# A recurrence in chunks and an ELU MLP on one core: the fourth pair of k heads rides in the unused rows of the other three tiles, so six transposes turn k and not eight

## The chip, the cores and the metric

The kernel runs on one core of a Trainium2 chip. The metric is device microseconds of one execution, from three runs of the kernel before; smaller is better. A profile was taken of one further execution.

## What is computed

The reference, cut to what matters. For each batch and head a 48 x 48 state is carried over 768 tokens; its output goes through a two-layer MLP with an ELU between.

```
B, H, S, D = 4, 8, 768, 48
f = 1 / (1 + exp(-f_logit))
for t in range(S):
    state = f[:, :, t, :, None] * state + einsum('bhd,bhe->bhde', k[:, :, t], v[:, :, t])
    y[:, :, t] = einsum('bhd,bhde->bhe', q[:, :, t], state)
x = y.transpose(0, 2, 1, 3).reshape(B * S, H * D)        # 3072 x 384
h = x @ w_in                                             # 384 -> 2048
out = where(h > 0, h, exp(min(h, 0)) - 1) @ w_out        # 2048 -> 384
```

q, k and f_logit lie in memory with tokens innermost, v with heads next to each other.

## The kernel before

The function `fast` does all the work here; `general` is a fallback that a flag selects, and it is not entered. The tokens are cut into 12 **units** of 256 (three to a batch). A unit passes through two parts: its attention, and sixteen **steps** of MLP. The MLP is the backbone of the program: 12 times 16 steps run in one written-out order (the loop at L1164), where an even step T computes a product with `w_in` (`up`, in `up7` at L883 seven-product form, matmuls at L893) and an odd step a product with `w_out` (`down`, matmuls at L995) for the block two behind. A table `plan` says which pieces of attention are put at which step. TensorE gets its instructions in exactly this order, and so do VectorE, ScalarE, GpSimd and the DMA queue of SP: `manual_schedule` leaves nothing to a scheduler, only the semaphore waits are derived.

**The tiles of q, k and f.** Eight heads of 48 rows make four pairs, and `qkf` holds a tile of 128 partitions x 4 pairs x 256 tokens for each of q, k and f, in two buffers used by alternate units. A pair fills 96 of 128 rows: rows 16 to 111 (`MAIN`); rows 0 to 15 and 112 to 127 (`GAP`) of a pair are unused and zero in q and k. For f the fourth pair is not loaded into a tile of its own at all: its 96 rows are put into the gap rows of the first three pairs (L441), so that the sigmoids, running products and reciprocals take three pairs of 256 columns and not four, and a DMA (`move`, L639) brings the fourth pair's decay to its own place afterwards.

**The pieces of attention of unit u**, with t = 16 (u - 1) as the step where the unit before it starts its MLP:

- `load` (L432) at t - 16: SP issues f, two f gap loads, k, q and v.
- `gates` at t - 8: two activations on ScalarE over f.
- `decays` (L641) at t - 7, t - 5, t - 3: VectorE makes the running product (`grow`, L627) and its reciprocal (`fall`, L632) of pair p, and GpSimd multiplies k and q by them (`scale`, L622, one instruction for each pair of q or k). `settle` at t - 1 does q of the third pair and k and q of the fourth.
- `transposed` (L663) at t + 2: TensorE turns the scaled k, 128 x 128 at a time: four pairs x two windows of 128 tokens, eight transposes (L670), into two PSUM tiles of two pairs each; ScalarE copies each tile to SBUF with one instruction of 128 x 512 (`kn`, L674).
- `both` at t + 5: `advance` (L729) multiplies turned k by v for the state updates, `scores` (L706) multiplies k by q; VectorE masks the scores (L714) and adds up the states (L687).
- `outputs` (L744) at t + 9 and `carried` (L764) at t + 11 make y. Between them ScalarE reads one column of each output bank (`between`, L751), and `carried` waits for that read. ScalarE then copies y to `xt` (L771, L773).

Units 0 and 1 go through a special start, while weights are still being unpacked. Unit 2 has steps of its own: decays at 16, 18, 20 and 22, the transposes at 23, `advance` at 25, `scores` at 26, `outputs` at 27, `carried` at 28; at the same steps VectorE builds combinations of `w_out` (`combine`, L861) for the seven-product form.

At step 4 `warm` (L1050) issues `SMALL` = 16 matmuls of one column each, whose result nobody reads.

An `elu` of a block (L947 on VectorE, then four sums on GpSimd, L957) is issued one block later than its `up`; ScalarE copies one quarter of each `up` product out of PSUM (`u`, L900), VectorE adds it to others (`hh`, L902, L915), and ScalarE takes two activations of the sum (`gg`, L925, L926).

Of the kernel before, what the change touches and what calls it, by code (L numbers as in the profile page):

```python
# [8 lines left out]
FP32 = mybir.dt.float32  # L9
# [347 lines left out]
def fast(ctx: ExitStack, tc: tile.TileContext, q, k, v, f_logit, w_in, w_out, out, flag, outer):  # L357
# [18 lines left out]
    nc = tc.nc  # L376
# [6 lines left out]
    NW = U // W  # L383
# [3 lines left out]
    HP = H // 2  # L387
    NFT = DFF // 128
    NKT = DM // 128
    PAD = 64 - D  # L390
# [5 lines left out]
    WA = 1  # L396
    F1 = (1, 3)
    W0 = 3
    SMALL = 16
    RR = 2  # L400
    HOLD = 2
    A1 = (2, 8, 10, 11)
# [10 lines left out]
    FULL = (slice(0, 64), slice(64, 128))  # L413
    MAIN = slice(PAD, 64 + D)
    GAP = (0, 64 + D)
    assert (D, DM, HP) == (48, 384, NKT + 1) and S % U == 0

    cst = ctx.enter_context(tc.tile_pool(name="cst", bufs=1))
    sb = ctx.enter_context(tc.tile_pool(name="sb", bufs=2))
    ps = ctx.enter_context(tc.tile_pool(name="ps", bufs=1, space=bass.MemoryType.PSUM))  # L420

    NB = 2

    qkf = [
        {n: cst.tile([128, HP, 2, U] if n == "f" else [128, HP, U], FP32, name=f"{n}{i}") for n in "fqk"}
        for i in range(NB)
    ]
    src = {"q": q, "k": k, "f": f_logit}
    vs = [cst.tile([128, NW, PAD + DM + PAD], FP32, name=f"v{i}") for i in range(NB)]
    ats, kns, xts, sts, pys = {}, {}, {}, {}, {}  # L430

    def load(u, names="fkqv"):  # L432
        b, s0 = u // UPB, (u % UPB) * U
        for n in names.replace("v", ""):
            to = qkf[u % NB][n][MAIN]
            frm = src[n][b, :, :, s0 : s0 + U].rearrange("(p r) d s -> (r d) p s", r=2)
            if n == "f":
                to, frm = to[:, 0:NKT, 0], frm[:, 0:NKT]
            nc.sync.dma_start(out=to, in_=frm)
            for r in range(2 if n == "f" else 0):  # L440
                nc.sync.dma_start(  # L441
                    out=qkf[u % NB][n][GAP[r] : GAP[r] + PAD, 0:NKT, 0],
                    in_=src[n][b, 2 * NKT + r, :, s0 : s0 + U].rearrange("(i j) s -> i j s", i=PAD),
                )
        if "v" in names:
            nc.sync.dma_start(
                out=vs[u % NB][:, :, PAD : PAD + DM], in_=v[b, s0 : s0 + U].rearrange("(c t) n -> t c n", t=W)
            )
# [16 lines left out]
    blank(0, nc.vector, nc.gpsimd)  # L465
    blank(1, nc.vector, zeros=nc.gpsimd)
    load(0, "fkq")
    load(1, "f")
    load(0, "v")

    fine = cst.tile([128, NKT, 1], FP32, name="fine")
    nc.vector.memset(fine[:], 1.0)
    first_y = [ps.tile([128, NW, NKT, C], FP32, tag="h", name=f"psY0_{b}", bufs=2) for b in range(2)]
    for y in first_y:
# [7 lines left out]
        out=causal[:], in_=causal[:], compare_op=ALU.is_ge, fill=0.0, base=0,  # L482
# [178 lines left out]
    pts = {}  # L661

    def transposed(u, h, bank, pairs=(0, 1)):  # L663

        if 0 in pairs:
            pts[u, h] = ps.tile([128, 2, NW, 128], FP32, tag=bank, name=f"psT{u}_{h}")
            kns[u, h] = sb.tile([128, 2, NW, 128], FP32, tag="kn", name=f"kn{u}_{h}")
        for p in pairs:
            for w in range(NW):
                nc.tensor.transpose(  # L670
                    pts[u, h][:, p, w], in_=qkf[u % NB]["k"][:, 2 * h + p, w * W : (w + 1) * W], identity=ident[:]
                )
        p = slice(pairs[0], pairs[-1] + 1)
        nc.scalar.copy(kns[u, h][:, p], pts[u, h][:, p])  # L674

    pus = {}

# [41 lines left out]
    def advance(u, pairs=range(HP)):  # L719

        if u not in pus:
            pus[u] = [ps.tile([128, NW, HP, D], FP32, tag=n, name=f"psU{u}_{n}") for n in ("a0", "a1")]
        pu = pus[u]
        for p in pairs:
            for w in range(NW):
                for r in range(2):
                    h = 2 * p + r
                    for b in range(2):
                        nc.tensor.matmul(  # L729
                            pu[b][FULL[r], w, p], lhsT=kns[u, p // 2][FULL[b], p % 2, w, FULL[r]],  # L730
                            rhs=vs[u % NB][FULL[b], w, PAD + h * D : PAD + (h + 1) * D],
                            start=(w == 0 and p == 0), stop=(w == NW - 1 and p == HP - 1), skip_group_check=True,
                        )
# [91 lines left out]
    def at_step(step, *todo):  # L825
        plan.setdefault(step, []).extend(todo)

    def both(u):

        advance(u)  # L830
        mask(u, scores(u, ("m3", "m0")))
        for c in range(NC):
            step(u, c)

    def attention(u, first, then):

        kept = []
        for p, i in enumerate(first):
            at_step(i, (lambda: settle(u)) if p == NKT else lambda p=p: decays(u, p))
        if u > 1:  # L840
            at_step(then[0], lambda: transposed(u, 0, "a0"), lambda: transposed(u, 1, "a1"))
        if len(then) == 4:
            at_step(then[1], lambda: both(u))
        else:
            at_step(then[1], lambda: advance(u))
            at_step(then[2], *(lambda c=c: step(u, c) for c in range(NC)))
            at_step(then[3], lambda: kept.append(scores(u)), lambda: mask(u, kept[0]))
        at_step(then[-2], lambda: outputs(u))
        at_step(then[-1], lambda: carried(u))
# [196 lines left out]
    def warm(n, bank="m0", small=0):  # L1046

        pw = ps.tile([128, 4, 128], FP32, tag=bank, name="psW")
        for _ in range(small):
            nc.tensor.matmul(pw[0:1, 0, 0:1], lhsT=ident[:, 0:1], rhs=ident[:, 0:1], start=True, stop=True)  # L1050
        for _ in range(n):
            nc.tensor.matmul(  # L1052
                pw[:], lhsT=ident[:], rhs=ident[:].unsqueeze(1).broadcast_to([128, 4, 128]), start=True, stop=True
            )
# [8 lines left out]
    for p in range(NKT):  # L1063
        grow(0, p)
        scale(0, ("k", p, nc.gpsimd))
        if p < 2:
            transposed(0, 0, "m0", (p,))
    move(0, 0, nc.scalar)
    transposed(0, 1, "m1", (0,))
    fall(0, 0)  # L1070
    scale(0, ("q", 0, nc.gpsimd))
    warm(WA, "m3")
    gates(1, bias=0)
    advance(0, (0, 1))
    pc = scores(0, ("m2", "m3"), (0,))
    nc.gpsimd.tensor_copy(
# [18 lines left out]
    a = qkf[1]["f"][:, 0:NKT, 0]  # L1095
# [33 lines left out]
    for n in range(1, NFT):  # L1129
        t = min(max(needs[n][0] - 2, 0), n)  # L1130
# [7 lines left out]
    at_step(A1[0], lambda: transposed(1, 0, "a0"), lambda: transposed(1, 1, "a1"))  # L1138
    at_step(4, lambda: warm(0, "m3", SMALL))
    attention(1, (), A1)  # L1140
# [10 lines left out]
    for u in range(3, NU):  # L1151
        t = (u - 1) * NFT
# [5 lines left out]
    for n in range(NR):  # L1158
        t = 3 * NFT + (NU - 4) * NFT * n // NR + RR
# [29 lines left out]
def kernel(tc, q, k, v, f_logit, w_in, w_out, out):  # L1189

    nc = tc.nc
    with tc.tile_pool(name="flags", bufs=1) as pool:
        flag = pool.tile([1, 1], I32, name="flag")
        store = fast(tc, q, k, v, f_logit, w_in, w_out, out, flag, pool)
        seen = nc.values_load(flag[0:1, 0:1])
        with tc.If(seen < 128) as branch:
            general(tc, q, k, v, f_logit, w_in, w_out, out)  # L1200
        with branch.Else():
            store(nc.sync, nc.scalar)
# [32 lines left out]
```

## Time and profile before

| What | Value |
|---|---|
| Three runs | 565.10, 565.82, 567.58 us; median 565.82 us |
| The profiled execution's own time | 565.24 us |
| Its span, first to last instruction | 563.5 us (1.74 us lie around it) |
| PE busy (matmul) | 544.1 us, 97% of the span |
| PE weight loads | 508.7 us, 90% |
| DVE, ACT, POOL busy | 407.1, 228.7, 293.5 us (72%, 41%, 52%) |
| Granted TensorE clock | 0.998 |

PE is TensorE, PEld its weight loads, DVE VectorE, ACT ScalarE, POOL GpSimd and SP the engine that issues most DMAs. A line of the groups names the line of the kernel, engine, operation, output and inputs, shape, count, busy microseconds, mean nanoseconds of one instruction, and the idle time of the engine ahead of them with what ended it. Matmuls are pipelined: each is shown longer than the distance to the next one's start, so the cost of a matmul in a dense stream is read from start to start in the timeline. In a timeline line the two numbers ahead are the start and the length, in microseconds, of a run of like instructions, and the count is at its end; a bracket tells of idle time ahead of it and what ended that.

### The profile page before, as it was taken

What the parts mean: (1) busy time and instruction counts of PE and PEld (TensorE: products, weight loads), DVE (VectorE), ACT (ScalarE), POOL (GpSimd) and SP (SyncE); (2) the same over time, 40 slices, a digit from 0 to 9 for tenths busy, and PEclk for the clock granted to TensorE, in tenths of its full rate; (3) what the DMA queues carried; (4) which work ended last, traced back from release to release, by engine and by line L of the source; (5) the groups of instructions that cost most, each with busy time, mean ns of one, the idle gap of its engine ahead of it and who ended that gap; (6) DMA issues with size and microseconds to landing.
All of it is one profiled execution on the core that took longest, in us unless ns stands there. A gap on an engine that the chain in (4) does not pass through costs nothing.

```text
span 563.5 us, 15590 instructions
## 1 busy us (share of the span) xinstructions
PE 544.1 (97%) x6368; PEld 508.7 (90%) x6368; DVE 407.1 (72%) x802; ACT 228.7 (41%) x424; POOL 293.5 (52%) x567
## 2 busy tenths in 40 slices
PE   7789898999999999999999999999999999999995
PEld 3466677999999999999999999999999999999995
DVE  8789989786676785785785785786686777735553
ACT  3279752434343433434334343343333343333331
POOL 6610779475374374465366367257257348325332
PEclk9999999999999999999999999999999999999999
DMA  8999951024024216216207307307306302201001
GB/s 209 257 250 231 288 150 43 3 52 111 2 51 140 59 33 170 73 20 179 79 10 182 87 10 183 85 9 183 86 9 181 88 9 71 86 4 33 30 2 35
DMA packets 38194, 53.31 MB, mean 95 GB/s; under 512 B 3712, under 2 KB 27936, under 8 KB 38112
## 3 DMA queue, kind: packets, MB, share of 16 engines
q1 hardware_dynamic: 37312, 51.62, 35.6%
q8 instruction: 52, 0.85, 0.6%
q10 hardware_dynamic: 800, 0.59, 0.5%
q14 instruction: 30, 0.25, 0.2%
HBM read 44.04 MB, written 4.72 MB: 87 GB/s over the span
## 4 chain that ended last, share of the span: by engine, by line
PE 84%; DVE 8%; ACT 3%; issue 3%; POOL 1%; DMA 1%; ACTq 0%; DVEq 0%; POOLq 0%
PE psH L893 37%; PE psM L995 36%; PE psU_a L729 2%; PE psS L706 2%; PE psY L744 2%; PE psY L764 2%; PE psT L670 2%; DVE f L632 2%; ACT area L574 1%; PE psW L1052 1%; DVE bits L564 1%; DMA f<-f 1%; DVE area L568 1%; PE psY L809 1%; DVE wi L582 1%
## 5 line engine op out<-in xcount | busy, mean ns | idle before, releaser
L893 PE MATMUL psH<-xt,wi 128*128 128x128 f32 (+1 forms) x1056 | 195.0, 294 | 0.0
L957 POOL TENSOR_TENSOR sums<-gg 128x128 f32<-128x128 f32 x176 | 78.3, 466 | 209.8 <-DVE gg L947 183.8
L925 ACT ACTIVATE gg<-hh 128x512 f32<-128x512 f32 x88 | 55.5, 630 | 252.3 <-DVE hh L915 117.5
L893 PEld LDWEIGHTS psH<-xt,wi 128*128 128x128 f32 x1056 | 149.5, 192 | 1.7 <-DVE hh L902 0.2
L893 PE MATMUL psH<-xt,area 128*128 128x128 f32 x704 | 121.8, 275 | 1.0 <-DVE hh L915 0.7
L893 PEld LDWEIGHTS psH<-xt,area 128*128 128x128 f32 x704 | 106.5, 191 | 6.1 <-PE psH L893 1.1
L902 DVE TENSOR_TENSOR hh<-psH,u 128x256 f32<-128x256 f32 x88 | 37.0, 420 | 101.3 <-ACT u L900 101.3
L995 PE MATMUL psM<-area,sums 128*128 128x192 f32 x528 | 102.2, 326 | 0.0
L995 PEld LDWEIGHTS psM<-area,sums 128*128 128x128 f32 x528 | 88.0, 190 | 0.2 <-issue 0.2
L995 PE MATMUL psM<-wo,gg 128*128 128x192 f32 x352 | 73.9, 332 | 0.0
L947 DVE SCALAR_TENSOR_TENSOR gg<-gg,hh 128x512 f32<-128x512 f32 x88 | 64.1, 728 | 1.5 <-ACT gg L926 1.5
L632 DVE RECIPROCAL f<-f 128x256 f32<-128x256 f32 x36 | 62.8, 1748 | 1.1
L926 ACT ACTIVATE gg<-gg 128x512 f32<-128x512 f32 x96 | 60.6, 631 | 3.0
L995 PEld LDWEIGHTS psM<-wo,gg 128*128 128x128 f32 x352 | 56.2, 190 | 1.4
L915 DVE TENSOR_TENSOR hh<-psH,u43h 128x256 f32<-128x256 f32 (+1 forms) x176 | 54.7, 353 | 3.0
L622 POOL TENSOR_TENSOR q<-q,f 128x256 f32<-128x256 f32 x48 | 38.9, 812 | 21.7 <-DVE f L632 8.7
L957 POOL TENSOR_TENSOR sums<-gg,sums 128x128 f32<-128x128 f32 x88 | 46.3, 527 | 6.9
L622 POOL TENSOR_TENSOR k<-k,f 128x256 f32<-128x256 f32 x48 | 40.5, 847 | 7.7 <-DMA f<-f 5.5
L957 POOL TENSOR_TENSOR sums<-sums,gg 128x128 f32<-128x128 f32 x88 | 43.9, 498 | 0.0
L915 DVE TENSOR_TENSOR u43h<-psH,hh 128x256 f32<-128x256 f32 x88 | 37.0, 420 | 8.9 <-PE psH L893 7.9
L995 PE MATMUL psM<-wo,sums 128*128 128x192 f32 x176 | 43.1, 326 | 0.0
L995 PE MATMUL psM<-area,gg 128*128 128x192 f32 x176 | 43.0, 326 | 0.0
(99 smaller groups left out, 646.9 us busy)
## 6 DMA issues: line engine op xcount, KB each, us to landing
area<-in_moe_w_out_dram SPq DMA_DIRECT2D x8, 768.0 KB, 10.1
again<-in_moe_w_in_dram SPq DMA_DIRECT2D x16, 384.0 KB, 3.8
again<-in_moe_w_out_dram SPq DMA_DIRECT2D x16, 384.0 KB, 3.7
k<-in_k_dram SPq DMA_DIRECT2D x12, 384.0 KB, 4.9
q<-in_q_dram SPq DMA_DIRECT2D x12, 384.0 KB, 5.8
v<-in_v_dram SPq DMA_DIRECT2D x12, 384.0 KB, 6.1
area<-in_moe_w_in_dram SPq DMA_DIRECT2D x8, 576.0 KB, 8.9
out_dram<-o SPq DMA_DIRECT2D x42, 96.0 KB, 1.7
```

The lines of the kernel that those rows point to most:

```text
L622: e.tensor_tensor(out=t[n][:, p], in0=t[n][:, p], in1=t["f"][:, p, "kq".index(n)], op=ALU.mult)
L632: nc.vector.reciprocal(f[:, p, 1], f[:, p, 0])
L670: nc.tensor.transpose(pts[u, h][:, p, w], in_=qkf[u % NB]["k"][:, 2 * h + p, w * W : (w + 1) * W], identity=ident[:])
L706: nc.tensor.matmul(pc[r][FULL[b], w, p], lhsT=t["k"][FULL[r], p, cols], rhs=t["q"][FULL[r], p, cols], start=True, stop=True,)
L893: nc.tensor.matmul(to, lhsT=lhs, rhs=rhs, start=(n == 0), stop=True, skip_group_check=True)
L902: add = lambda to, x, y: nc.vector.tensor_tensor(out=to, in0=x, in1=y, op=ALU.add)
L915: add = lambda to, x, y: nc.vector.tensor_tensor(out=to, in0=x, in1=y, op=ALU.add)
L925: nc.scalar.activation(g[:], h, AF.Relu, scale=-1.0)
L926: nc.scalar.activation(g[:], g[:], AF.Exp, scale=-1.0)
L947: nc.vector.scalar_tensor_tensor(out=g[:], in0=g[:], scalar=-1.0, in1=phs.pop(P), op0=ALU.add, op1=ALU.max)
L957: nc.gpsimd.tensor_tensor(out=s[:, i], in0=x, in1=y, op=op)
L995: nc.tensor.matmul(pm[bank][:, half * DH : (half + 1) * DH], lhsT=x, rhs=y, start=first, stop=(j == NP - 1), skip_group_check=True,)
```

## The change

For units 2 to 11 the load of k also puts the fourth pair's 96 rows into the gap rows of the first three pairs, as f has it (heads 6 and 7, 48 rows each, 16 x 3 x 256 values to each side), besides the fourth pair's own tile, which `scores` still reads. The scaling of the first three pairs by f then scales those rows too. `transposed` turns only the first three pairs (two windows each). The turned k is now one tile `kn` for all units; after each copy of turned pairs a second ScalarE copy takes the gap columns out of the same PSUM tile and spreads them into the fourth pair's place, every third column. `SMALL` goes from 16 to 21. Units 0 and 1 keep eight transposes.

```diff
-    SMALL = 16
+    SMALL = 21
...
+    kn = cst.tile([128, HP, NW, 128], FP32, name="kn")
...
-            for r in range(2 if n == "f" else 0):
+            for r in range(2 if n == "f" or n == "k" and u > 1 else 0):
+                gap = qkf[u % NB][n][GAP[r] : GAP[r] + PAD, 0:NKT]
                 nc.sync.dma_start(
-                    out=qkf[u % NB][n][GAP[r] : GAP[r] + PAD, 0:NKT, 0],
+                    out=gap[:, :, 0] if n == "f" else gap,
                     in_=src[n][b, 2 * NKT + r, :, s0 : s0 + U].rearrange("(i j) s -> i j s", i=PAD),
                 )
...
     def transposed(u, h, bank, pairs=(0, 1)):
+        pairs = [p for p in pairs if u < 2 or 2 * h + p < NKT]
         if 0 in pairs:
             pts[u, h] = ps.tile([128, 2, NW, 128], FP32, tag=bank, name=f"psT{u}_{h}")
-            kns[u, h] = sb.tile([128, 2, NW, 128], FP32, tag="kn", name=f"kn{u}_{h}")
         for p in pairs:
             for w in range(NW):
                 nc.tensor.transpose(
                     pts[u, h][:, p, w], in_=qkf[u % NB]["k"][:, 2 * h + p, w * W : (w + 1) * W], identity=ident[:]
                 )
-        p = slice(pairs[0], pairs[-1] + 1)
-        nc.scalar.copy(kns[u, h][:, p], pts[u, h][:, p])
+        p, to = slice(pairs[0], pairs[-1] + 1), slice(2 * h + pairs[0], 2 * h + pairs[-1] + 1)
+        nc.scalar.copy(kn[:, to], pts[u, h][:, p])
+        if u < 2:
+            return
+        gaps = kn[:, NKT, :, MAIN].rearrange("t w (r i j) -> t j w r i", r=2, j=NKT)
+        nc.scalar.copy(gaps[:, to], pts[u, h][:, p].rearrange("t p w (a i) -> t p w a i", i=PAD)[:, :, :, 0::7])
...
-                            pu[b][FULL[r], w, p], lhsT=kns[u, p // 2][FULL[b], p % 2, w, FULL[r]],
+                            pu[b][FULL[r], w, p], lhsT=kn[FULL[b], p, w, FULL[r]],
```

Set against each other engine by engine, the two programs differ in this and in nothing else: TensorE has 2 transposes fewer in each of ten units and 5 one-column matmuls more; ScalarE has, in each of those units, copies of 128 x 512, 128 x 128, 128 x 256 and 128 x 64 in place of two of 128 x 512; SP has two more loads of k in each; VectorE and GpSimd have the same instructions in the same order. In the steady units TensorE's wait for GpSimd's scaling of the fourth pair moves from the seventh transpose to a later instruction.

More of the change, by code (lines that the diff above doesn't have):

```diff
@@ L429, in fast @@
     vs = [cst.tile([128, NW, PAD + DM + PAD], FP32, name=f"v{i}") for i in range(NB)]
-    ats, kns, xts, sts, pys = {}, {}, {}, {}, {}
+    kn = cst.tile([128, HP, NW, 128], FP32, name="kn")
+    ats, xts, sts, pys = {}, {}, {}, {}
     def load(u, names="fkqv"):
```

## The prediction

> **What bounds the kernel now.** I read the page's chain first, to learn which engine ends last, then the groups by shape for the prices, then TensorE's waits, then the timeline around the transposes.
>
> ```profile
> PE 84%; DVE 8%; ACT 3%; issue 3%; POOL 1%; DMA 1%; ACTq 0%; DVEq 0%; POOLq 0%
> ```
>
> TensorE carries 84% of the chain that ended last. The groups price the operations concerned:
>
> ```profile
> L670 PE MATMUL psT<-ident,k 128*128 128x128 f32 x96 | 13.2, 275 | 1.9 <-POOL k L622 1.4 <-ACT kn L674 0.6
> ...
> L900 ACT COPY u<-psH 128x128 f32<-128x128 f32 x88 | 23.0, 261 | 39.2 <-PE psH L893 39.1
> L674 ACT COPY kn<-psT 128x512 f32<-128x512 f32 x22 | 11.9, 591 | 1.5 <-PE psT L670 1.5
> L674 ACT COPY kn<-psT 128x256 f32<-128x256 f32 x4 | 1.5, 373 | 8.3 <-PE psT L670 7.2 <-PE psW L1052 1.2
> ```
>
> 96 transposes are busy for 13.2 us although each is shown as 275 ns: they overlap, so the mean is not their price. The timeline of TensorE at the transposes of unit 3 gives it:
>
> ```profile
> 128.55 0.49 PE L995 MATMUL psM<-wo,sums 128*128 128x192 f32 x2
> 128.88 1.04 PE L670 MATMUL psT<-ident,k 128*128 128x128 f32 x8
> 129.75 0.39 PE L893 MATMUL psH<-xt,wi 128*128 128x128 f32 x2
> ```
>
> Eight transposes start at 128.88 and the next matmul at 129.75, with no bracket: 0.87 us / 8 = **0.109 us** each, in a stream without a gap. After 97.6 us the timeline of TensorE shows no idle bracket in any unit, so from unit 3 on the program's length is the sum of such distances. At unit 2 it is otherwise:
>
> ```profile
> 95.91 0.82 PE L670 MATMUL psT<-ident,k 128*128 128x128 f32 x6
> 97.60 0.44 PE L670 MATMUL psT<-ident,k 128*128 128x128 f32 x2 [0.88 <-POOL k L622]
> 97.88 0.82 PE L995 MATMUL psM<-wo,gg 128*128 128x192 f32 x4
> ```
>
> Here the fourth pair's two transposes wait for GpSimd's scaling of the fourth pair (96.38 + 1.17 = 97.55 us): the eight take 97.88 - 95.91 = 1.97 us.
>
> **What the Trainium skill says.** "TensorE: Matmul & The Clock Gate", Part 4: PE-mode transpose, gives about 275 ns for a 128 x 128 transpose inside a kernel; the trace's mean agrees as a length, but 109 ns from start to start is what one costs here, and I use that. "Perfetto Trace Analysis", Per-engine timelines, says that a matmul's end is estimated and not observed: a second reason to count from start to start. "ScalarE: Activation LUTs", What ACT_TABLE_LOAD costs, gives 186 ns + 0.833 ns an element for an instruction with immediates and an overlap of some 93 ns between neighbours; for 512 elements that is an estimate of 613 ns against 591 in the trace, for 128 one of 293 against 261, so the trace is a little cheaper and is used.
>
> **The change part by part.**
>
> *Transposes, units 3 to 11.* Nine units lose two each, inside a dense stream: 9 x 2 x 0.109 = **1.96 us** gained. What could be late next in that stretch? The sums that the next `down` reads: GpSimd ends those at 131.33 us and the matmuls that read them start at 132.84. Turned k is ready at 130.6 and is first read at 137.00. Both have over 1 us, so 0.22 us earlier is harmless.
>
> *Transposes, unit 2.* Six would take 0.65 us, so TensorE moves on 1.97 - 0.65 = 1.31 us earlier. I don't book that, because another chain runs beside it. ScalarE is busy without a gap from 97.99 to 102.01 (two activations, the turned k, two gate activations, u); VectorE waits for that u, then has no idle bracket from 102.04 to 115.1; and ScalarE waits for VectorE's hh:
>
> ```profile
> 102.04 0.42 DVE L902 TENSOR_TENSOR hh<-psH,u 128x256 f32<-128x256 f32 x1 [2.67 <-ACT u L900]
> ...
> 111.01 0.62 DVE L915 TENSOR_TENSOR hh<-psH,u43h 128x256 f32<-128x256 f32 x2
> ```
>
> ```profile
> 111.72 0.63 ACT L925 ACTIVATE gg<-hh 128x512 f32<-128x512 f32 x1 [2.93 <-POOL sums L957]
> 112.39 0.63 ACT L926 ACTIVATE gg<-gg 128x512 f32<-128x512 f32 x1
> 112.92 0.34 ACT L751 COPY between<-psY 128x8 f32<-128x8 f32 x2
> ```
>
> ```profile
> 113.53 1.16 PE L764 MATMUL psY<-q,state 64*64 64x64 f32 x64
> ```
>
> (The bracket names GpSimd at L925, but hh ends at 111.63, just ahead of 111.72.) `carried` starts at 113.53 and the `between` that it waits for ends at 113.26. In unit 1, where `carried` really waited, it started 0.07 us after the end of `between` (62.27 to 62.33). So it could have started at 113.33: of 1.31 us, only 0.2 can be kept past this point. On the way it shows first at `scores`, which waits for the state additions that end at 105.18 against its start at 106.24 (0.8 us left), then at `outputs`, behind the mask that ends at 109.24 against 109.97. Each wait is shorter than the one it replaces, and the last one gives nearly all back.
>
> *ScalarE's copies.* From start to start, two copies of 512 take 0.94 us at unit 2. An occupancy is the length less an overlap of 0.1 us: 512 takes 0.48, 128 takes 0.16, 256 takes 0.27, and 64 about 0.1 (from 155 ns at 8 elements and 261 at 128). The four sum to 1.01, 0.07 us more. The new ones write every third element, which no copy here shows. Nearest is the unpacking at L574 with strided reads and writes: 1938 ns for 768 elements, 2.5 ns each. At that price the gap copies take 0.36 and 0.2 us, together 0.37 us more than before. A gain is excluded: 64 elements fewer (0.06 us) stand against two more instructions. I take 0.1, bounds 0.05 and 0.37. In units 3 to 11 it is covered: the copies start at 129.51 and u is wanted at 130.84 - 0.22 = 130.62, so 1.01 fits and the worst price delays u by 0.2, while the bank that VectorE frees behind it (131.56) is wanted at 134.47, 2.9 us later. At unit 2 it lies on the chain above, so unit 2 gains 0.2 - 0.1 = **0.1 us** (from -0.17 to 1.31).
>
> *Loads.* Two more issues on SP in each of ten units; the like pair of f takes 1.2 to 1.9 us on SP and lands in 3.8 us. Queued behind are q and v of the same load, and after them stores. For unit 2 k is issued at 63.39 and GpSimd first multiplies it at 81.22; for unit 3 at 75.33 and 106.38. 18 to 31 us cover them: nothing. GpSimd's and TensorE's waits on more DMA semaphores are for events long past; in the trace such a wait instruction takes 51 ns in TensorE's queue, whose sequencer is ahead. Without that cover it is 10 x 0.05 = 0.5 us.
>
> *SMALL.* The 16 show as 32 records, 25 ns from start to start (35.12 to 35.90), so five more take 0.25 us. Behind them TensorE idles 1.20 us for VectorE's wi L582 until 37.26; covered. Without that cover, +0.25.
>
> Sum: 565.24 - 1.96 - 0.10 = **563.18 us** for the profiled execution. It lay 0.58 below the median of the runs shown, for which the same sum is 563.76. I forecast the middle, **563.5 us**.
>
> **The rivals.**
>
> *Unit 2 keeps its whole gain.* For it: the wait is in plain sight, TensorE is the bound. Against: the chain above, with 0.2 us in hand. 565.24 - 1.96 - 1.31 = 562.0, up to 562.5 on the median.
>
> *The steady units keep nothing*, because VectorE or GpSimd paces each unit and TensorE merely looks full. For: VectorE 72% busy. Against: in every unit VectorE idles some 3 us for u, which follows TensorE, and GpSimd up to 4.4 us for VectorE. 565.1.
>
> *Slower: the strided copies choke ScalarE.* One mechanism, at t + 2 of ten units: they hold up u, u holds up hh, hh holds a bank for the next `up`. With 2.9 us to spare it decides only once the copies take about 4 us in place of 1.1; each 0.5 us beyond costs 5 us in ten units, hence a loss beyond 0.5%, about 569. It needs 18 ns an element, seven times the slowest strided row here.
>
> *The change doesn't do what it says*: excluded by the instruction order, which has six transposes.
>
> **How the numbers follow.** Forecast (563.2 to 563.8) 0.71, unit 2 kept 0.15, nothing kept 0.10, slower 0.04. A difference of 0.5% (2.8 us) is about what a measurement of this kernel can tell from no change. The runs before spread over 2.5 us, so a gain of 2.1 can appear as over 2.8: I add 0.05 of the forecast's chance to the kept case and get faster 0.20, same 0.75, slower 0.05. The range, 562.0 to 565.1, takes in the unit 2 bound, most of the no-gain case, and the scatter; it leaves out the slower case and the edges.
>
> **What would show it.** Right: six transposes in about 0.65 us in every unit; the distance between transposes of neighbouring units down from 43.40 to 43.18 us; the 0.88 us wait at 97.60 gone, and in its place short waits at `scores` and `outputs` of unit 2, or at `carried` for `between`, which starts at about 113.4. Wrong: `carried` of unit 2 near 112.2 (unit 2 kept), a unit distance still 43.40 with new brackets on TensorE (another pace), or ScalarE's gap copies over 0.5 us each with u late.

## The result and the profile after

The changed kernel takes 562.76 us in the median of 7 runs (561.71 to 564.59), the kernel before, run beside it, 566.12 us (565.10 to 567.91, 7 runs). The ratio is **0.9942**, with a 95% interval of 0.9925 to 0.9959. The same kernel was timed twice more beside the kernel before and gave 0.9953 both times (0.9939 to 0.9967, and 0.9936 to 0.9970), so the gain is near half a per cent. Two executions of the kernel before, beside the first repetition, took 936 and 3180 us where its others took 565 to 567; they are not counted. The profiled execution took 562.76 us, with a span of 561.0 us; before, it was 565.24 and 563.5. The two traces thus differ by 2.47 us and the medians by 3.36; both lie in the interval, which is a gain of 2.3 to 4.2 us.

The chain of the page of the changed kernel still lies on TensorE, with about the share that it had:

```profile
PE 82%; DVE 7%; DMA 6%; issue 2%; ACT 1%; SPq 0%; POOL 0%; DVEq 0%; ACTq 0%; POOLq 0%
```

The groups by shape of the changed kernel show what replaced what: 76 transposes in place of 96, and ScalarE's four copies to a unit (the two of L680 are the new ones, which take the gap columns and write every third element):

```profile
L672 PE MATMUL psT<-ident,k 128*128 128x128 f32 x76 | 10.7, 274 | 1.0 <-POOL k L624 1.0
...
L676 ACT COPY kn<-psT 128x256 f32<-128x256 f32 x14 | 5.4, 385 | 8.5 <-PE psT L672 7.3 <-PE psW L1058 1.2
...
L680 ACT COPY kn<-psT 128x128 f32<-128x128 f32 x10 | 3.4, 342 | 0.0
L680 ACT COPY kn<-psT 128x64 f32<-128x64 f32 x10 | 2.7, 268 | 0.0
```

A strided copy of 128 columns is 342 ns long where the plain one of 128 (L900 before) had 261: 81 ns more. Its length is not its cost, as the timeline of ScalarE at unit 2 shows:

```profile
99.03 0.57 ACT L676 COPY kn<-psT 128x512 f32<-128x512 f32 x1
99.50 0.34 ACT L680 COPY kn<-psT 128x128 f32<-128x128 f32 x1
99.66 0.39 ACT L676 COPY kn<-psT 128x256 f32<-128x256 f32 x1
99.94 0.25 ACT L680 COPY kn<-psT 128x64 f32<-128x64 f32 x1
100.04 0.86 ACT L615 ACTIVATE f<-f 128x768 f32<-128x768 f32 x1
```

The strided 128 occupies 99.66 - 99.50 = 0.16 us, the strided 64 0.10 us, and the four together 100.04 - 99.03 = 1.01 us.

In the steady part, TensorE's timeline at unit 3 has six transposes in the place of eight, and no bracket behind them. They take 129.22 - 128.56 = 0.66 us, 0.110 each:

```profile
128.24 0.49 PE L1001 MATMUL psM<-wo,sums 128*128 128x192 f32 x2
128.56 0.82 PE L672 MATMUL psT<-ident,k 128*128 128x128 f32 x6
129.22 0.39 PE L899 MATMUL psH<-xt,wi 128*128 128x128 f32 x2
```

At unit 2 the wait of 0.88 us for GpSimd is gone. Three others stand on the way to `carried`; the last line is the first product behind it:

```profile
95.86 0.82 PE L672 MATMUL psT<-ident,k 128*128 128x128 f32 x6
96.52 0.82 PE L1001 MATMUL psM<-wo,gg 128*128 128x192 f32 x4
```

```profile
105.20 1.16 PE L712 MATMUL psS<-q,k 64*64 64x64 f32 x64 [0.25 <-PE psM L1001]
...
108.92 1.44 PE L750 MATMUL psY<-at,v 64*64 64x64 f32 x64
...
113.04 1.34 PE L770 MATMUL psY<-q,state 64*64 64x64 f32 x64 [0.20 <-ACT between L757]
114.31 0.38 PE L899 MATMUL psH<-xt,wi 128*128 128x128 f32 x1
```

The mask on VectorE, which `outputs` waits for, and the two reads on ScalarE, which `carried` waits for:

```profile
107.94 1.22 DVE L720 TENSOR_TENSOR at<-psS,twice 128x512 f32<-128x512 f32 x2
```

```profile
112.84 0.34 ACT L757 COPY between<-psY 128x8 f32<-128x8 f32 x2
```

`scores` and `carried` have a bracket; `outputs` has none, but its 64 matmuls are shown as 1.44 us where 64 like them take 1.16 without a stop: the wait lies inside the run.

**Where the time went.** I compare the two traces at fixed instructions. The lead of the changed kernel, in us, is the earlier start of the same instruction:

| at | before | after | lead |
|---|---|---|---|
| first transpose of unit 2 | 95.91 | 95.86 | 0.05 |
| first product behind `carried` of unit 2 | 114.62 | 114.31 | 0.31 |
| last matmul | 557.55 | 555.32 | 2.23 |
| end of the span | 563.51 | 561.04 | 2.47 |

Between the second row and the third the lead grows by 1.92 us, in nine steps of about 0.21: the transposes of neighbouring units lie 43.18 to 43.24 us apart, before it was 43.40 to 43.41. Unit 2 gave 0.26. The last 0.24 came behind the last matmul, where no instruction was changed.

### The profile page after: what moved, and what is told of

Its sections match the earlier page's. It is cut to its first block, busy times and chain, and to the rows that moved or that the text cites. A ratio compares the mean times of both kernels' runs of the same rounds, so it can differ in the third digit from the quotient of the medians.

```text
span 561.0 us, 15626 instructions
## 1 busy us (share of the span) xinstructions
PE 542.0 (97%) x6358; PEld 507.3 (90%) x6358; DVE 406.0 (72%) x802; ACT 229.2 (41%) x444; POOL 292.6 (52%) x567
## 4 chain that ended last, share of the span: by engine, by line
PE 82%; DVE 7%; DMA 6%; issue 2%; ACT 1%; SPq 0%; POOL 0%; DVEq 0%; ACTq 0%; POOLq 0%
PE psH L899 37%; PE psM L1001 36%; DMA area<-in_moe_w_in_dram 3%; PE psY L750 2%; PE psY L770 2%; PE psU_a L735 2%; PE psS L712 2%; DVE f L634 2%; DMA f<-in_f_logit_dram 1%; PE psT L672 1%; DMA f<-f 1%; DMA xt<-xt 1%; DVE bits L566 1%; DVE f L629 1%; DVE wo L584 1%
```

## The experiments

The theory that the prediction stood on: from unit 3 on a transpose is worth its distance in a dense stream, and at unit 2 a chain through ScalarE and VectorE gives most of the removed wait back. The rivals: the saving comes from, or is eaten by, one of the additions (loads, copies, the single tile, `SMALL`); or the unit is paced by another engine. Every kernel was timed in alternation with the kernel before; ratios are to that. To take out the start of the program, which scatters, the traces are measured from the first transpose of unit 2, called T2:

| kernel | ratio (95%) | distance of units 3 and 4 | `carried` - T2 | last matmul - T2 | last matmul to end |
|---|---|---|---|---|---|
| before | 1 | 43.40 | 17.62 | 461.64 | 5.97 |
| after | 0.9942 (0.9925 to 0.9959) | 43.18 | 17.17 | 459.46 | 5.71 |
| after again | 0.9953 (0.9939 to 0.9967) | 43.18 | 17.19 | 459.43 | 5.44 |
| after, third time | 0.9953 (0.9936 to 0.9970) | 43.18 | 17.28 | 459.57 | 5.50 |
| `SMALL` = 16 | 0.9953 (0.9941 to 0.9966) | 43.18 | 17.28 | 459.52 | 5.43 |
| before with `SMALL` = 21 | 0.9997 (0.9988 to 1.0006) | 43.40 | 17.53 | 461.70 | 6.17 |
| gates later | 0.9955 (0.9943 to 0.9968) | 43.18 | 17.30 | 459.70 | 5.55 |
| eight transposes | 0.9982 (0.9969 to 0.9995) | 43.40 | 17.52 | 461.75 | 5.50 |
| eight again | 0.9990 (0.9978 to 1.0002) | 43.40 | 17.62 | 461.79 | 5.53 |
| no gap copies | 0.9932 (0.9908 to 0.9956) | 43.18 | 17.00 | 459.45 | 5.90 |
| four transposes | 0.9891 (0.9867 to 0.9914) | 42.96 | 16.90 | 457.31 | 5.62 |
| decays later | 0.9908 (0.9887 to 0.9930) | 43.18 | 16.31 | 458.43 | 5.46 |
| before, one tile | 1.0008 (0.9997 to 1.0019) | 43.40 | 17.51 | 461.79 | 6.20 |
| before, decays later | 1.0000 (0.9988 to 1.0012) | 43.40 | 17.52 | 461.63 | 5.86 |

Later units have the same distances, apart from one or two in most traces that are 0.03 to 0.17 us longer, with six transposes and with eight. So the same work scatters by some 0.2 us from T2 to the last matmul (461.63 to 461.79 with eight transposes).

The ratios of the kernels without gap copies, with four transposes and with later decays lie 0.26 to 0.28% below what their traces give from T2 to the end (0.9960, 0.9917 and 0.9934). They were timed beside the same runs of the kernel before, of which the first ten have a median of 567.1 us and the other fourteen one of 565.6. The likely reason is this scatter of the yardstick; what these kernels are worth is read from the traces.

**The changed kernel again**, without an edit, as a control.

> The changed kernel once more, as the control that the three kernels beside it are read against. Theory A (the gain is TensorE's stream: 18 transposes of 0.109 us in units 3 to 11, and 0.2 to 0.3 us kept at unit 2, 2.2 us in all): 0.4% faster than before, ratio 0.996. Theory B (SMALL's five more one-column matmuls carry another 1 us by way of the start): ratio 0.994, as first measured. Theory C (the kernel ends the same work later by chance of the start, the ratio of 0.9942 is a draw out of a scatter of 2.5 us): anything from 0.993 to 0.998, with 0.996 inside the interval.

Measured: 562.85 us, 0.9953. From T2 to the last matmul the trace agrees with that of the first execution within 0.03 us.

**`SMALL` alone**, taken back in the changed kernel:

```diff
-    SMALL = 21
+    SMALL = 16
```

> The changed kernel with SMALL back at 16. Theory A: the fillers end some 1.2 us before VectorE's weights release TensorE, so nothing changes: within 0.3 us of the control. Theory B: about 1 us slower than the control, the ratio to before near 0.996.

Measured: 0.9953, the same as the control.

**`SMALL` alone, added to the kernel before:**

```diff
-    SMALL = 16
+    SMALL = 21
```

> The kernel before with SMALL at 21 and nothing else. Theory A: ratio 1.000, the first product behind the fillers still starts at about 37.26 us. Theory B: some 1 us faster, ratio 0.998.

Measured: 0.9997. In its trace the product behind the one-column matmuls still waits 1.18 us for wi (1.20 in the kernel before), so five more of them are covered.

**The gates of unit 3 one step later**, in the changed kernel. It was to take two activations of 0.9 us out of ScalarE's way to u:

```diff
-        at_step(t - 8, lambda u=u: gates(u))
+        at_step(t - (7 if u == 3 else 8), lambda u=u: gates(u))
```

> The changed kernel with one edit: the gates of unit 3 (two activations, 1.65 us on ScalarE) one step later, at 25 and not 24, so that they stand behind the copy of u and not ahead of it. Theory A (at unit 2 the gain is held back by the chain ScalarE u, VectorE hh to mask and hh, ScalarE between): u starts near 100.0 us and not 101.68, the short waits of scores, outputs and carried in unit 2 go, carried starts near 112.2 and not 113.04, and the whole is about 0.8 to 1.0 us faster than the control, ratio to before near 0.9945 if the control is at 0.996. Rival (the chain starts elsewhere: VectorE is simply full from 102 us on): carried within 0.2 us of 113.04 and the time unchanged.

Measured: 0.9955, nothing gained. The timeline of this kernel says why:

```profile
100.07 0.29 ACT L906 COPY u<-psH 128x128 f32<-128x128 f32 x1
...
104.59 0.84 ACT L617 ACTIVATE f<-f 128x768 f32<-128x768 f32 x1
105.52 0.69 DVE L629 TENSOR_TENSOR_SCAN f<-f 128x256 f32<-128x256 f32 x1 [1.39 <-issue]
...
106.31 1.75 DVE L634 RECIPROCAL f<-f 128x256 f32<-128x256 f32 x1
```

```profile
107.98 1.22 DVE L720 TENSOR_TENSOR at<-psS,twice 128x512 f32<-128x512 f32 x2
```

u does come 1.6 us earlier (100.07 in place of 101.68). But unit 3's running product (L629) now waits for the later gates, and it stands, with its reciprocal, ahead of unit 2's mask in VectorE's order; the mask starts at 107.98 as it did (107.94), and `carried` at 113.09. The chain had been named at the wrong place: u was one entry, the order on VectorE another.

**Two transposes put back**, everything that the change adds left in. The gap rows are then turned twice, once by themselves and once in the fourth pair's tile, whose result is not read:

```diff
+        turned = pairs
         pairs = [p for p in pairs if u < 2 or 2 * h + p < NKT]
...
-        for p in pairs:
+        for p in turned:
```

> The changed kernel with the two transposes of the fourth pair put back on TensorE in units 2 to 11; nobody reads what they write. The loads, the four copies and SMALL stay as changed, so this is the change's cost without its gain. Theory A (the gain is the 20 transposes, the additions are covered): unit distance 43.40 us again, ratio to before 1.000 within 0.001, and the wait for GpSimd at unit 2 back. Rival (part of the gain comes from elsewhere in the change, as the single turned-k tile or other waits): ratio still below 0.998, unit distance below 43.40. Rival (the copies or loads cost in the steady units and the gain hides it): ratio above 1.001, unit distance above 43.42.

Measured: 0.9982 (0.9969 to 0.9995). The transposes of units 2 and 3 in its timeline:

```profile
97.77 0.44 PE L673 MATMUL psT<-ident,k 128*128 128x128 f32 x2 [0.78 <-POOL k L624]
...
129.05 1.04 PE L673 MATMUL psT<-ident,k 128*128 128x128 f32 x8
```

The wait at unit 2 is back, and the unit distance is 43.40 again. From T2 to the last matmul it takes 461.75 us, the time before. Of the gain of 0.18% (0.05 to 0.31%, or 0.3 to 1.8 us) the trace shows some 0.4 us, behind the last matmul. **The same kernel in another set of runs:**

> The changed kernel with the two transposes put back, once more. Theory A: ratio 1.000 within 0.001. Rival (some 1 us of the measured gain lies in the additions, in the start that a trace from unit 2 doesn't cover): 0.998 again.

Measured: 0.9990 (0.9978 to 1.0002), 461.79 us from T2 to the last matmul. Up to the last matmul the additions cost nothing that these runs can tell, and the removal of two transposes gives all of the gain. Behind it the additions seem to gain a little; that is taken up below.

**The gap copies left out**, six transposes kept. The fourth pair's turned k is then never written, so the states of heads 6 and 7 are not those of the reference:

```diff
-        gaps = kn[:, NKT, :, MAIN].rearrange("t w (r i j) -> t j w r i", r=2, j=NKT)
-        nc.scalar.copy(gaps[:, to], pts[u, h][:, p].rearrange("t p w (a i) -> t p w a i", i=PAD)[:, :, :, 0::7])
```

> The changed kernel without the two copies that spread the gap columns; the fourth pair of turned k then stays what unit 1 left, so the states of heads 6 and 7 are not the reference's. It takes 0.26 us (0.16 and 0.10, start to start) off ScalarE at unit 2. Theory A (at unit 2 a chain over ScalarE and VectorE holds TensorE): carried of unit 2 starts about 0.26 us earlier, near 112.8 us, the next product likewise; steady units stay at 43.19; the whole 0.05% faster than the changed kernel, less than the timing resolves. Rival (the copies are covered everywhere, unit 2 included): carried stays near 113.04.

Measured: 0.9932 (0.9908 to 0.9956), which can't be told from the changed kernel. In its trace the two remaining copies take 101.14 - 100.41 = 0.73 us in place of 1.01, and the way from the first activation ahead of them to `between` takes 14.73 us (99.21 to 113.94) in place of 15.00 (97.84 to 112.84). So the gap copies do lie on unit 2's chain. `carried` comes 0.17 to 0.28 us nearer to T2 than in the three executions of the changed kernel, as was expected; at the last matmul nothing is left of it (459.45 against 459.43 to 459.57). A gain of 0.2 us at one unit is at the edge of what these traces can follow.

**Four transposes**: two more left out in each of the ten units, with the copies that read them; a part of the turned k stays stale, so the output is not the reference's.

```diff
         pairs = [p for p in pairs if u < 2 or 2 * h + p < NKT]
+        if u > 1 and h:
+            return
```

> The cause doubled: of units 2 to 11 only the first two pairs are turned and copied, so the third pair and a third of the fourth stay stale and the output is not the reference's. Four transposes and not six. Theory A: unit distance falls by a further 2 x 0.109 to 42.97 us, nine such units give 1.96 us more, unit 2 gives no more than the 0.2 us that the shorter copies free, so about 2.0 to 2.2 us below the changed kernel, ratio to before near 0.9915. Rival (another engine is near to being the pace of the steady units): unit distance above 43.0 and new brackets on TensorE.

Measured: 0.9891, 560.82 us. The timeline at unit 3:

```profile
128.77 0.60 PE L674 MATMUL psT<-ident,k 128*128 128x128 f32 x4
129.21 0.39 PE L901 MATMUL psH<-xt,wi 128*128 128x128 f32 x2
```

Four take 0.44 us, and the unit distance falls by another 0.22, to 42.96. From T2 to the last matmul it takes 2.15 us less than the changed kernel. Each transpose is worth 0.11 us, these two as much as the two before: down to four transposes, nothing but TensorE paces the units from 3 on.

**The decays of unit 3 later as well**, in the changed kernel. After the failure of the gates alone, both the gates and unit 3's first running product and reciprocal were moved, the latter by two steps, behind unit 2's mask:

```diff
-        at_step(t - 8, lambda u=u: gates(u))
-        attention(u, [t + i for i in D3], [t + i for i in A3])
+        at_step(t - (7 if u == 3 else 8), lambda u=u: gates(u))
+        attention(u, [t + (-5 if u == 3 and i == -7 else i) for i in D3], [t + i for i in A3])
```

> The changed kernel with two moves for unit 3 alone: its gates one step later (as in the kernel that moved only those) and its first decays at 27 and not 25, behind the hh of the block. What the earlier move left: the running product and reciprocal of unit 3 stood ahead of the mask on VectorE and waited for the gates, so mask, outputs and carried came no sooner. Theory A (VectorE's order ahead of the mask holds unit 2): no wait of TensorE at scores, outputs or carried of unit 2, carried near 112.0 us (113.04 in the changed kernel), about 1.0 us below the changed kernel, ratio to before near 0.9935 if the changed kernel is at 0.9953. Rival (ScalarE's or GpSimd's backlog then takes the place): carried within 0.3 us of 113.04, or a new wait of like size in the blocks up to 135 us.

Measured: **561.33 us** (560.92 to 563.05), 0.9908 (0.9887 to 0.9930): faster than both kernels. By the traces, counted from T2, it is 3.2 us ahead of the kernel before at the last matmul and 1.0 ahead of the changed one, as was expected. `outputs` and `carried` of unit 2 in its timeline, and VectorE's mask:

```profile
108.13 1.16 PE L750 MATMUL psY<-at,v 64*64 64x64 f32 x64
...
111.69 1.16 PE L770 MATMUL psY<-q,state 64*64 64x64 f32 x64
```

```profile
105.61 1.29 DVE L720 TENSOR_TENSOR at<-psS,twice 128x512 f32<-128x512 f32 x2 [1.89 <-PE psS L712]
...
108.69 0.62 DVE L921 TENSOR_TENSOR hh<-psH,u43h 128x256 f32<-128x256 f32 x2
```

Neither has a bracket any more, nor has `scores`, and both runs are 1.16 us long. VectorE now waits 1.89 us for `scores`, where `scores` and `outputs` waited for VectorE; hh comes at 108.69 in place of 110.92. `carried` is 17.62 - 16.31 = 1.31 us nearer to T2 than in the kernel before. That is what the removed wait and the two transposes of unit 2 had freed. Gates and decays were moved together; whether the decays alone would do was not tried.

**The same moves in the kernel before:**

> The kernel before with the two moves of unit 3 (gates one step later, first decays at 27) and eight transposes. Theory A (the moves pay only where TensorE comes early to unit 2, and before it came late because of the transposes' own wait): the wait of 0.88 us at the transposes of unit 2 stays, carried within 0.1 us of where it was against those transposes (17.6 us behind their start), ratio 1.000. Rival (VectorE's order held the kernel before as well): carried earlier by over 0.3 us, ratio near 0.998.

Measured: 1.0000 (0.9988 to 1.0012). In its timeline the transposes wait as before:

```profile
97.57 0.44 PE L670 MATMUL psT<-ident,k 128*128 128x128 f32 x2 [0.78 <-POOL k L622]
...
113.49 1.16 PE L764 MATMUL psY<-q,state 64*64 64x64 f32 x64
```

There GpSimd's scaling of the fourth pair sets the time of unit 2, and a freer VectorE has nothing to give. At unit 2 the two edits are worth nothing and some 0.2 us alone and 1.3 together: two limits in a row.

**One tile for turned k**, alone in the kernel before (two copies to one tile, in place of tiles from a pool):

```diff
-            kns[u, h] = sb.tile([128, 2, NW, 128], FP32, tag="kn", name=f"kn{u}_{h}")
...
-        p = slice(pairs[0], pairs[-1] + 1)
-        nc.scalar.copy(kns[u, h][:, p], pts[u, h][:, p])
+        p, to = slice(pairs[0], pairs[-1] + 1), slice(2 * h + pairs[0], 2 * h + pairs[-1] + 1)
+        nc.scalar.copy(kn[:, to], pts[u, h][:, p])
```

> The kernel before with one turned-k tile for all units in place of two buffers, and nothing else. Asked because the kernel with eight transposes and all additions was timed at 0.9982 of before though its trace from unit 2 to the end is 0.1 us longer. Theory A (that is scatter of the start): ratio 1.000, unit distance 43.40. Rival (the tile's place or waits in the start give up to 1 us): ratio near 0.9985.

Measured: 1.0008 (0.9997 to 1.0019); nothing that can be told.

**The changed kernel a third time:**

> The changed kernel as a control on this chip. Theory A: ratio 0.996, from 0.994 to 0.997.

Measured: 563.87 us, 0.9953. This profiled execution had a late start (T2 at 98.48 us); from there on it is the same as the others within 0.15 us. The start is taken up below.

## Why the prediction was right, and where it was off

The forecast was 563.5 us, with 562.0 to 565.1 as its range; the median was 562.76. The direction, the main term and the mechanism at unit 2 were right. Step by step:

- **Transposes, units 3 to 11, 1.96 us.** Measured 1.92 in the pair of traces. The price of 0.109 us was read from start to start; four transposes give the same price (0.110), so the stream is dense there, and no other engine comes next. The rival in which the steady units keep nothing is ruled out by the unit distances of 43.40, 43.18 and 42.96.
- **Transposes, unit 2, 0.1 us.** Measured 0.26 in the pair of traces. From T2 to the product behind `carried` the six kernels with eight transposes take 18.60 to 18.71 us, the three executions of the changed kernel and the one with `SMALL` = 16 take 18.45 to 18.56, so in the mean it is 0.14, near the forecast. All three waits that were named came, at `scores`, `outputs` and `carried`, the last at 113.04 against "about 113.4". The rival of 1.31 us is ruled out for this kernel, and the later decays show what it lacked: with VectorE's order changed, all of the 1.31 is kept.
- **How `carried` waits was read wrongly, and two errors cancel.** The prediction let it wait for the end of both reads of `between` (113.26 before). The 62.27 that it takes from unit 1 is the end of the first read; the second ended at 62.48, after `carried` had begun. So it is in unit 2: its first matmul starts 0.05 us behind the first read's end (112.98), its fifth 0.05 behind the second's (113.18). It could start earlier than forecast, 0.40 us before 113.53 and not 0.2, but is stretched from 1.16 to 1.34. The product behind it had 0.40 - 0.18 = 0.22 us in hand, the forecast's 0.2; that this number came out is in part luck. The slack of `scores` was misread too: 106.24 - 105.18 is 1.06 us, not 0.8, and its wait of 0.25 is 1.31 - 1.06. In the pair of traces the chain itself ran 0.08 us earlier at its end, although the copies took 0.07 more, because its first activation started at 97.84 in place of 97.99; what moved that activation was not tried.
- **What holds unit 2.** The prediction gave ScalarE's gapless row, u, and VectorE's gapless row behind it. The gates moved alone show that this was incomplete: the decay of unit 3 on VectorE is enough to hold it without u.
- **ScalarE's copies, 0.1 us (0.05 to 0.37).** Four copies take 1.01 us, as the sum said, 0.07 more than the two before. The Trainium skill ("ScalarE: Activation LUTs", What ACT_TABLE_LOAD costs) gives an overlap of some 93 ns between activations that follow each other; the trace agrees for plain copies (0.57 long, 0.47 from start to start). The strided ones, for which no run had a price before, overlap by 0.15 to 0.18: their additional 81 ns is length, not occupancy. The upper bound, from the 16-bit unpacking of L574, was the wrong row for it. (The 155 ns at 8 elements are 162 in the groups, which changes nothing.)
- **Loads, 0.** Right, and the cover was used: for unit 2 the added issues stand at 65.24 and 68.37, where those of q and v stood before (65.46 and 68.41). Each takes SP 0.56 us; between them SP stands still, as it did before. So q went out at 71.47 and v at 71.83. The later of the added loads landed at 71.76, some 8 us before GpSimd first multiplies that unit's k, and no wait of TensorE or GpSimd for q or v of unit 2 shows.
- **`SMALL`, 0.** Right, from both sides.
- **The missing term.** The sum was 563.18 for the profiled execution, which took 562.76. Of these 0.42 us, about 0.16 are unit 2, and some 0.25 lie behind the last matmul, where the prediction had nothing. There the nine traces with the added loads and gap copies take 5.43 to 5.71 us, the four without the loads 5.86 to 6.20, and the kernel without gap copies 5.90. That kernel seems not to fit, but its last store landed late, 4.71 us behind the last matmul, where the others have 4.2 to 4.6. From the last landing of a store to the end of the span the four kernels without the added loads take 1.59 to 1.63 us, and the nine with them whose trace has that landing take 1.13 to 1.25, the one without gap copies 1.20. So 0.4 us go with the added loads in every trace, about what the eight-transpose kernels gain behind the last matmul. The traces also show that the landing of the last four stores is signalled by other semaphores: without the added loads by the four that SP waits for last in its closing row of eight waits, with them by the four that it waits for first. That this is the reason was not tried; it stays open.

The weakest part was the chance. The working put the gain at 2.1 us, 0.37%, and gave 0.75 to "within 0.5%" and 0.20 to "faster by over 0.5%". Measured were 0.58% at first, on the side that had 0.20, with an interval of 0.41 to 0.75%, and 0.47% twice after it; the pair of traces gives 0.44%. The small terms, 0.16 us at unit 2 and 0.25 to 0.4 at the end, were enough to carry a gain of 0.37% near that edge, and the scatter of the runs did the rest.

## What to carry to other kernels

In a stream without gaps, an operation was worth its distance from start to start here (0.11 us), however long its record is (0.27 us). A wait that is removed is worth only the slack of the chain that is late next, so look at what is queued, in order, ahead of that chain's instructions on each engine: here the gates and one running product of the next unit, queued ahead of this unit's u and mask, held back 1.0 of 1.3 us. Two limits in a row show nothing when only one is lifted; after the first is gone, place the side work of the other engines anew.

## What the runs showed of the hardware that was not expected

The start of the program scatters: in three executions of the changed kernel T2 lay at 95.86, 95.81 and 98.48 us, and 2.7 of the 2.9 us between the spans of the last two (560.7 and 563.6) come from it. It goes with TensorE's granted clock: of the fourteen traces, the ten with none or one stretch at half the clock ahead of T2 have it at 95.21 to 96.18 us, the three with two such stretches at 96.34 to 97.13, and this one, with three, at 98.48. The row of the page for the changed kernel's third time, and two of its stretches (the columns are the stretch, its length, busy time and count of PE, PEld, DVE, ACT and POOL, then the granted clock, the DMA share and GB/s):

```profile
PEclk8989899999999999999999999999999999999999
```

```profile
38.58:41.99 3.41, 3.41 (x9) 2.69 (x10) 3.38 (x6) 3.38 (x6) 0.00 (x0) 0.50 1.04 227
41.99:65.88 23.89, 21.59 (x322) 16.31 (x321) 23.03 (x38) 19.57 (x19) 7.06 (x9) 1.00 0.96 265
```

For 3.41 us the clock is 0.50, and TensorE gets through 9 matmuls; the same stretch of the control has a clock of 1.00 and 14. There are three such stretches, from 11.27, 38.58 and 65.88 us, 27.3 us apart. The Trainium skill ("TensorE: Matmul & The Clock Gate", Part 1) describes a free-running window of 3413 ns at half the clock or the whole, and the length agrees; that half the clock follows an idle window doesn't show here, where TensorE's longest idle time in the 3.4 us ahead of 38.58 is 0.95 us. Most of a single drop near 39 us is hidden: twelve products take 4.51 us in place of 2.83, and the wait of 1.26 us, which the control has behind the next eight, disappears. A change of this size is better read from a fixed instruction behind the start than from two whole executions.
